# One core, decode attention for two caches: K queued one unit ahead of V, p.v two chunks behind the scores

## The chip, the cores and the metric

The kernel runs on one core of one Trainium2 chip. The metric is device time in microseconds: before, the median of three runs is 870.74 (870.53 to 872.84). The engines meant below are PE (matmul; PEld is its weight load), DVE (vector), ACT (scalar) and SP, which here only issues DMA transfers. A profile of one execution gives every instruction's start and duration, every DMA packet, and who released whom.

## The reference

Two attention blocks for a single query token, A over the whole cache and B over its last 4096 keys; their output rows are laid side by side:

```python
def _A_ref(x, k_cache, v_cache, wq, wo):          # x [1,1,512], caches [1,32,16384,128]
    q = (x @ wq).reshape(B, Sq, Hq, Dh).transpose(0, 2, 1, 3)
    scores = jnp.einsum("bhqd,bhkd->bhqk", q, k) * (Dh ** -0.5)
    p = softmax(scores, axis=-1)
    o = jnp.einsum("bhqk,bhkd->bhqd", p, v)
    return o.transpose(0, 2, 1, 3).reshape(B, Sq, Hq * Dh) @ wo
# _B_ref: the same with k_cache[:, :, Sk - W:], v_cache[:, :, Sk - W:], W = 4096
```

There are 32 heads of 128 in both, each with its own K and V. In bf16 one head of A has 4 MB of K and 4 MB of V, one head of B 1 MB of each; each wq and each wo has 4 MB. Every byte of K and V is used once.

## The kernel before

**Units and chunks.** The work is cut into 40 units. A unit is one head of A or four heads of B, so that it always has 128 keys on each of the 128 partitions: 4 MB of K and 4 MB of V. After every four heads of A comes the unit of B with the same four heads. A unit has two chunks of 64 keys a partition (U = 64); a chunk of B has two pieces, one for each of its two heads.

**Work on one chunk.** `_mult` (L144, DVE) multiplies K with the broadcast query into `prod`. `_add` (L156, DVE) adds the two halves of the head dimension. `_red` (L169, PE, eight matmuls with an identity) sums those further into PSUM. `_softmax` reduces the last eight columns (L181, DVE) and takes the exponential with its sum (L185, ACT). `_pv` (L201, PE) runs 64 small matmuls of p with V, and one with the sums (L210). When a head is through, its "fins" follow: reciprocal (L225, DVE), scaling (L227, ACT), a turn into a column (L239, PE), and after every fourth head a cast (L250, DVE) and the four matmuls with wo (`_fin_out`, L256, PE).

**Order on the engines.** Each engine runs its instructions in program order. The main loop emits for chunk c: the multiply of c, the softmax of c-1, the add of c, fins of earlier heads, the red of c, and then the p.v of chunk c-1. From the last two chunks on, p.v is put off: those of the last three chunks follow the red of the last one, with fins between.

**Order of the transfers.** All large loads are issued by SP, in the order of one list, `_Loads`, which emits the next load once its pool has a free buffer in program order. On the chip SP waits at the head of the queue until the readers of the buffer's old contents are done; all that is listed behind waits too. There are two buffers for K (`kt`, which also take both wq), two for V (`vt`), two for wo. A buffer of K is given back by the unit's second multiply, one of V by the p.v of its second chunk, one of wq by the q matmuls (L99), one of wo by `_fin_out` of its eighth head. The list runs

```
wqA, K0, V0, woA(0), K1, V1, K2, V2, wqB, woB(0), K3, V3, K4, V4, ...
```

so K and V of a unit stand together. A wo tile holds 1 MB for eight heads; A's is listed behind V of head 0, 8, 16, 24, B's behind V of A's head 2, 10, 18, 26. At the end K of the last unit, which is B's, goes ahead of the last V of A, and the last of the four V transfers of that unit is cut in two. x of A and of B is loaded on ACT's queue (L78), and DVE broadcasts both (L81) before its first multiply. The chunk with number 6 is preceded by the q matmuls of B.

Of the kernel before, what the change touches and what calls it, by code (L numbers as in the profile page):

```python
# [9 lines left out]
BF16 = mybir.dt.bfloat16  # L10
P = 128
# [5 lines left out]
G = 4  # L17
# [52 lines left out]
class _Unit:  # L70
    kt = vt = None
# [9 lines left out]
        cx.o(nc.vector.tensor_copy(st.xb[:, c, :], xT[:, c : c + 1].broadcast_to([P, P])))  # L81


def _load_wq(nc, cx, st):
    D, N = st.wq.shape
    KC = D // P
    st.wq_t = cx.kt_pool.tile([P, KC, N], BF16, tag="kt", name="wq_t")
    cx.o(nc.sync.dma_start(out=st.wq_t[:, :, :], in_=st.wq.rearrange("(p c) f -> p c f", c=KC)))


def _q(nc, cx, st):

    D, N = st.wq.shape
    KC = D // P
    st.qall = cx.singles.tile([P, N], BF16, tag=f"qall{st.name}", name=f"qall{st.name}")
    for j in range(N // 512):
        q_ps = cx.red_pool.tile([P, 512], F32, tag="red", name="q_ps")
        for c in range(KC):
            cx.o(nc.tensor.matmul(  # L99
                q_ps[:, :],  # L100
                lhsT=st.xb[:, c, :],
                rhs=st.wq_t[:, c, j * 512 : (j + 1) * 512],
                start=(c == 0),
                stop=(c == KC - 1),
            ))
        cx.o(nc.scalar.copy(st.qall[:, j * 512 : (j + 1) * 512], q_ps[:, :]))  # L106
    cx.loads.release("kt")


def _load_wo(nc, cx, st, i):  # L110

    t = cx.wo_pool.tile([P, 2, G * st.DN], BF16, tag="wo", name="wo_t")
    st.wo_t[i] = t
    n = 2 * G * DH
    cx.o(nc.sync.dma_start(  # L115
        out=t[:, :, :],
        in_=st.wo[i * n : (i + 1) * n, :].rearrange("(g p j) f -> p g (j f)", g=2, j=G),
    ))


def _load_kv(nc, cx, unit, which, cut_last=1):
    pool, tag = (cx.kt_pool, "kt") if which == "k" else (cx.vt_pool, "vt")
    t = pool.tile([P, unit.keys, DH], BF16, tag=tag, name=tag)
    setattr(unit, tag, t)
    st = unit.st
    view = st.k_view if which == "k" else st.v_view
    L = st.W // P
    n = len(unit.heads)
    for i, h in enumerate(unit.heads):
        src = view[h].rearrange("(p l) d -> p l d", p=P)  # L130
        cuts = cut_last if i == n - 1 else 1
        w = L // cuts
        for c in range(cuts):
            cx.o(nc.sync.dma_start(  # L134
                out=t[:, i * L + c * w : i * L + (c + 1) * w, :],
                in_=src[:, c * w : (c + 1) * w, :],
            ))


def _mult(nc, cx, ch):  # L140
    ch.prod = cx.prod_pool.tile([P, U, DH], BF16, tag="prod", name="prod")
    for k0, n, st, h, _, _ in ch.pieces:
        q = st.qall[:, h * DH : (h + 1) * DH]
        cx.o(nc.vector.tensor_tensor(  # L144
            out=ch.prod[:, k0 : k0 + n, :],
            in0=ch.unit.kt[:, ch.k0 + k0 : ch.k0 + k0 + n, :],
            in1=q.rearrange("p (o d) -> p o d", o=1).broadcast_to([P, n, DH]),
            op=ALU.mult,
        ))
    if ch.last_of_unit:  # L150
        cx.loads.release("kt")


def _add(nc, cx, ch):
    ch.half = cx.half_pool.tile([P, U, DH // 2], BF16, tag="half", name="half")
    cx.o(nc.vector.tensor_tensor(  # L156
        out=ch.half[:, :, :],
        in0=ch.prod[:, :, 0 : DH // 2],
        in1=ch.prod[:, :, DH // 2 : DH],
        op=ALU.add,  # L160
    ))
# [16 lines left out]
def _softmax(nc, cx, ch):  # L178

    sc = cx.small.tile([P, U], F32, tag="sc", name="sc")  # L180
    cx.o(nc.vector.tensor_reduce(out=sc[:, :], in_=ch.red[:, :, :], axis=AX.X, op=ALU.add))  # L181
    ch.p = cx.small.tile([P, U], BF16, tag="p", name="p_sb")
    ch.cs = cx.small.tile([P, len(ch.pieces)], F32, tag="cs", name="cs")
    for i, (k0, n, _, _, _, _) in enumerate(ch.pieces):
        cx.o(nc.scalar.activation(  # L185
            out=ch.p[:, k0 : k0 + n],
            in_=sc[:, k0 : k0 + n],
            func=ACT.Exp,
            scale=SCALE,
            accum_out=ch.cs[:, i : i + 1],  # L190
        ))


def _pv(nc, cx, ch, i):

    k0, n, st, h, first, last = ch.pieces[i]
    if first:
        st.o_ps[h] = cx.pso_pool.tile([1, DH + 1], F32, tag="o", name="o_ps")
    o_ps = st.o_ps[h]
    for c in range(n):  # L200
        cx.o(nc.tensor.matmul(  # L201
            o_ps[0:1, 0:DH],
            lhsT=ch.p[:, k0 + c : k0 + c + 1],
            rhs=ch.unit.vt[:, ch.k0 + k0 + c, :],
            start=(first and c == 0),
            stop=(last and c == n - 1),
            skip_group_check=True,
        ))
        if c == 0:
            cx.o(nc.tensor.matmul(  # L210
                o_ps[0:1, DH : DH + 1],
                lhsT=ch.cs[:, i : i + 1],
                rhs=cx.ones_col[:, 0:1],
                start=False,
                stop=last,
                skip_group_check=True,
            ))
    if ch.last_of_unit and i == len(ch.pieces) - 1:
        cx.loads.release("vt")
# [52 lines left out]
def kernel(  # L272
# [14 lines left out]
    nc = tc.nc  # L287
# [4 lines left out]
    cx = _Ctx()  # L292
    cx.o = _Order(tc)
    cx.out = out
    pool = lambda name, bufs, **kw: ctx.enter_context(tc.tile_pool(name=name, bufs=bufs, **kw))
# [12 lines left out]
    ld = cx.loads = _Loads()  # L308
# [19 lines left out]
    def problem(name, x, k_cache, v_cache, wq, wo, sk0, W, at):  # L328
        st = _Problem()
        st.name, st.x, st.wq, st.wo, st.W, st.at = name, x, wq, wo, W, at  # L330
        st.H = k_cache.shape[1]
        st.DN = wo.shape[1]
        st.k_view = k_cache[0, :, sk0 : sk0 + W, :]
        st.v_view = v_cache[0, :, sk0 : sk0 + W, :]
        st.out_ps = cx.psout_pool.tile([1, st.DN], F32, tag=f"out{name}", name=f"out{name}")
        st.wo_t, st.o_ps, st.orow = {}, {}, {}
        return st

    stA = problem("A", A_x, A_k_cache, A_v_cache, A_wq, A_wo, 0, SkA, 0)
    stB = problem("B", B_x, B_k_cache, B_v_cache, B_wq, B_wo, SkB - WB, WB, A_wo.shape[1])  # L340


    units = []
# [4 lines left out]
    chunks = []  # L348
    for i, (st, heads) in enumerate(units):
        u = units[i] = _Unit()  # L350
# [4 lines left out]
        for k0 in range(0, u.keys, U):  # L355
            pieces, at = [], 0
            while at < U:
                h, off = heads[(k0 + at) // L], (k0 + at) % L
                n = min(U - at, L - off)
# [3 lines left out]
        chunks += u.chunks  # L363


    ld.add("kt", lambda: _load_wq(nc, cx, stA))
    n = len(units)
    for i, u in enumerate(units):
        if i < n - 1:
            ld.add("kt", lambda u=u: _load_kv(nc, cx, u, "k"))  # L370
        if i == n - 2:
            ld.add("kt", lambda: _load_kv(nc, cx, units[n - 1], "k"))
        ld.add("vt", lambda u=u, c=(2 if i == n - 1 else 1): _load_kv(nc, cx, u, "v", c))
        if i == G - 2:
            ld.add("kt", lambda: _load_wq(nc, cx, stB))
        per = 2 * G
        if u.st is stA and u.heads[0] % per == 0:
            ld.add("wo", lambda b=u.heads[0] // per: _load_wo(nc, cx, stA, b))
        if u.st is stA and u.heads[0] % per == 2:
            ld.add("wo", lambda b=u.heads[0] // per: _load_wo(nc, cx, stB, b))  # L380

    _load_x(nc, cx, stA)
    _load_x(nc, cx, stB)
# [3 lines left out]
    fins = []  # L387


    def fin_pe():  # L390
        for f in list(fins):
            s, st, h = f
            if s == 1:
                _fin_col(nc, cx, st, h)
                f[0] = 2 if h % G == G - 1 else 9
            elif s == 3:
                _fin_out(nc, cx, st, h)
                f[0] = 9
        fins[:] = [f for f in fins if f[0] != 9]

    def fin_dve():
        for f in fins:
            s, st, h = f
            if s == 0:
                _fin_row(nc, cx, st, h)
                f[0] = 1
            elif s == 2:
                _fin_cast(nc, cx, st, h)
                f[0] = 3

    def pv(ch):
        for i, (_, _, st, h, _, last) in enumerate(ch.pieces):
            _pv(nc, cx, ch, i)
            if last:
                yield [0, st, h]

    prev = None
    waiting = []
    tail_from = len(chunks) - 3
    for c, ch in enumerate(chunks):  # L420
        if c == 2 * (G - 1):
            _q(nc, cx, stB)
        _mult(nc, cx, ch)
        if prev is not None:
            _softmax(nc, cx, prev)
            waiting.append(prev)
        _add(nc, cx, ch)
        fin_dve()
        fin_pe()
        _red(nc, cx, ch)  # L430
        if c <= tail_from:
            while waiting:
                fins += pv(waiting.pop(0))
        prev = ch
    _softmax(nc, cx, prev)
    waiting.append(prev)
# [40 lines left out]
```

## Time and profile before

| what | value |
|---|---|
| median of three runs | 870.74 us |
| the profiled execution | 869.08 us |
| its span, first to last instruction | 867.4 us |
| granted TensorE clock, mean | 0.838 |
| busy: DVE, PE, PEld, ACT | 588.4, 567.8, 390.7, 64.8 us |
| HBM read | 352.32 MB |
| share of the 16 DMA engines that SP's transfers took | 95.9% |
| idle of DVE before the multiply, ended by A's K | 208.0 us |

A row of a group gives busy time, then the mean duration of one instruction in nanoseconds, then the idle time before it and who ended it. The row of a window gives its ends, the busy time of each engine, then the granted clock, the mean share of the DMA engines in use and GB/s; packets are counted where they start. "SPq" is SP's queue, an instruction there is the issue of a transfer. Times are counted from the span's start.

### The profile page before, as it was taken

The page shows a single profiled execution, that of the slowest core. Times are in us where ns is not written, and L with a number is a line of the kernel's source. Part 1 is how long each engine was busy: PE and PEld are TensorE (multiplying, and loading weights), DVE is VectorE, ACT ScalarE, POOL GpSimd, SP SyncE. Part 2 cuts the span into 40 slices and gives each one's busy share as a digit, 9 for nine tenths or more (in the row PEclk, how much of TensorE's full clock was granted, in tenths as well). Part 3 has the DMA queues.
Part 4 walks back from the last instruction along what each step waited for, and adds up shares of the span by engine and source line. Part 5 has one row for each costly group of instructions (what it writes and reads, how often), then busy time and mean ns, then how long its engine had stood idle before and what let it go on. Part 6 is the DMA issues. An engine that isn't in the chain of part 4 may idle for free.

```text
span 867.4 us, 13704 instructions
## 1 busy us (share of the span) xinstructions
PE 567.8 (65%) x6336; PEld 390.7 (45%) x6336; DVE 588.4 (68%) x344; ACT 64.8 (7%) x275; POOL 0.8 (0%) x8
## 2 busy tenths in 40 slices
PE   3466585766665765676855758577757575667678
PEld 1154263544443544444633536344544354444446
DVE  0666486769557695777865768666955769577791
ACT  2000200000010000100000000000001000010001
POOL 0000000000000000000000000000000000000000
PEclk9688897988977888888977879788897788888888
DMA  9999999999989999999989999999998999999980
GB/s 387 435 428 417 428 436 426 417 424 417 437 360 434 427 413 439 418 425 422 433 371 433 408 426 426 428 414 430 401 440 362 422 426 418 439 411 416 431 359 2
DMA packets 21389, 353.20 MB, mean 407 GB/s; under 512 B 2514, under 2 KB 2516, under 8 KB 4820
## 3 DMA queue, kind: packets, MB, share of 16 engines
q1 hardware_dynamic: 21044, 352.33, 95.9%
q8 instruction: 49, 0.80, 0.4%
q10 hardware_dynamic: 288, 0.00, 0.0%
q14 instruction: 8, 0.07, 0.0%
HBM read 352.32 MB, written 0.00 MB: 406 GB/s over the span
## 4 chain that ended last, share of the span: by engine, by line
DMA 56%; DVE 18%; PE 17%; issue 7%; SPq 1%; ACT 0%; DVEq 0%; ACTq 0%
DMA kt<-in_A_k_cache_dram 53%; PE o_ps L201 9%; DVE prod L144 9%; DVE half L156 7%; PE red L169 6%; DMA xTB<-in_B_x_dram 3%; DVE sc L181 2%; PE outB L256 2%; SPq L134 1%; PE outA L256 1%; SPq L115 0%; DVE oc L250 0%; PE oc_ps L239 0%; DVE recip L225 0%; PE o_ps L210 0%
## 5 line engine op out<-in xcount | busy, mean ns | idle before, releaser
L144 DVE TENSOR_TENSOR prod<-kt,qallA 128x8192 bf16<-128x8192 bf16 x64 | 283.0, 4422 | 208.6 <-DMA kt<-in_A_k_cache_dram 208.0
L201 PEld LDWEIGHTS <-p_sb 128*1 128x1 bf16 x5120 | 296.7, 85 | 42.8 <-issue 42.7
L201 PE MATMUL o_ps<-vt,p_sb 128*1 128x128 bf16 x5120 | 314.1, 222 | 1.7 <-DMA vt<-in_A_v_cache_dram 1.7
L169 PE MATMUL red<-half,ident 128*128 128x512 bf16 x640 | 203.2, 475 | 126.7 <-DVE half L156 126.7
L156 DVE TENSOR_TENSOR half<-prod 128x4096 bf16<-128x4096 bf16 x80 | 182.5, 2282 | 0.0
L169 PEld LDWEIGHTS <-ident 128*128 128x128 bf16 x640 | 68.4, 114 | 225.5 <-issue 178.9
L185 ACT ACTIVATE p_sb<-sc 128x64 bf16<-128x64 f32 (+1 forms) x96 | 23.5, 244 | 654.6 <-DVE sc L181 654.6
L144 DVE TENSOR_TENSOR prod<-kt,qallB 128x4096 bf16<-128x4096 bf16 x32 | 71.9, 2287 | 0.3
L181 DVE TENSOR_REDUCE sc<-red 128x64 f32<-128x512 f32 x80 | 54.8, 685 | 12.8 <-PE red L169 12.6
L256 PEld LDWEIGHTS <-oc 128*1 128x1 bf16 x64 | 5.3, 101 | 126.5 <-DVE oc L250 75.9
L256 PE MATMUL outA<-wo_t,oc 128*1 128x512 bf16 x32 | 14.1, 591 | 69.3 <-DVE recip L225 59.6
L256 PE MATMUL outB<-wo_t,oc 128*1 128x512 bf16 x32 | 14.1, 590 | 45.6 <-DVE oc L250 45.6
L239 PE MATMUL oc_ps<-one,orow 1*32 1x1 bf16 x256 | 16.3, 171 | 35.6 <-ACT orow L227 35.6
L239 PEld LDWEIGHTS <-orow 1*32 1x32 bf16 x256 | 11.5, 110 | 49.7 <-ACT orow L227 42.1
L227 ACT ACTIVATE orow<-o_ps,recip 1x128 bf16<-1x128 f32 x64 | 22.2, 357 | 111.0 <-DVE recip L225 111.0
L225 DVE RECIPROCAL recip<-o_ps 1x1 f32<-1x1 f32 x64 | 9.1, 150 | 28.4 <-PE o_ps L201 28.1
L210 PE MATMUL o_ps<-ones_col,cs 128*1 128x1 f32 x192 | 19.0, 168 | 0.0
L185 ACT ACTIVATION_READ_ACCUMULATOR p_sb<-sc 128x1 f32 x96 | 17.9, 186 | 0.0
L99 PE MATMUL q_ps<-wq_t,xbA 128*128 128x512 bf16 x32 | 8.4, 430 | 13.5 <-DVE xbA L81 13.5
L210 PEld LDWEIGHTS o_ps<-ones_col,cs 128*1 128x1 f32 x192 | 14.1, 87 | 1.7 <-issue 1.7
L99 PEld LDWEIGHTS <-xbA 128*128 128x128 bf16 x32 | 3.5, 108 | 18.0 <-DVE xbA L81 13.7
L99 PE MATMUL q_ps<-wq_t,xbB 128*128 128x512 bf16 x32 | 8.2, 378 | 4.7 <-ACT qallB L106 4.7
(17 smaller groups left out, 19.6 us busy)
## 6 DMA issues: line engine op xcount, KB each, us to landing
kt<-in_A_k_cache_dram SPq DMA_DIRECT2D x32, 4096.0 KB, 23.5
vt<-in_A_v_cache_dram SPq DMA_DIRECT2D x32, 4096.0 KB, 16.7
kt<-in_B_k_cache_dram SPq DMA_DIRECT2D x32, 1024.0 KB, 19.8
vt<-in_B_v_cache_dram SPq DMA_DIRECT2D x31, 1024.0 KB, 10.0
wq_t<-in_A_wq_dram SPq DMA_DIRECT2D x1, 4096.0 KB, 12.2
wo_t<-in_A_wo_dram SPq DMA_DIRECT2D x4, 1024.0 KB, 5.0
wq_t<-in_B_wq_dram SPq DMA_DIRECT2D x1, 4096.0 KB, 24.6
wo_t<-in_B_wo_dram SPq DMA_DIRECT2D x4, 1024.0 KB, 16.9
```

Source lines behind the costliest of these rows:

```text
L99: cx.o(nc.tensor.matmul(q_ps[:, :], lhsT=st.xb[:, c, :], rhs=st.wq_t[:, c, j * 512 : (j + 1) * 512], start=(c == 0), stop=(c == KC - 1),))
L144: cx.o(nc.vector.tensor_tensor(out=ch.prod[:, k0 : k0 + n, :], in0=ch.unit.kt[:, ch.k0 + k0 : ch.k0 + k0 + n, :], in1=q.rearrange("p (o d) ...
L156: cx.o(nc.vector.tensor_tensor(out=ch.half[:, :, :], in0=ch.prod[:, :, 0 : DH // 2], in1=ch.prod[:, :, DH // 2 : DH], op=ALU.add,))
L169: cx.o(nc.tensor.matmul(ch.red[:, :, :], lhsT=cx.ident[:, :], rhs=ch.half[:, :, b * W : (b + 1) * W], start=(b == 0), stop=(b == nb - 1),))
L181: cx.o(nc.vector.tensor_reduce(out=sc[:, :], in_=ch.red[:, :, :], axis=AX.X, op=ALU.add))
L185: cx.o(nc.scalar.activation(out=ch.p[:, k0 : k0 + n], in_=sc[:, k0 : k0 + n], func=ACT.Exp, scale=SCALE, accum_out=ch.cs[:, i : i + 1],))
L201: cx.o(nc.tensor.matmul(o_ps[0:1, 0:DH], lhsT=ch.p[:, k0 + c : k0 + c + 1], rhs=ch.unit.vt[:, ch.k0 + k0 + c, :], start=(first and c == 0) ...
L210: cx.o(nc.tensor.matmul(o_ps[0:1, DH : DH + 1], lhsT=ch.cs[:, i : i + 1], rhs=cx.ones_col[:, 0:1], start=False, stop=last, skip_group_chec ...
L225: cx.o(nc.vector.reciprocal(recip[:, :], o_ps[0:1, DH : DH + 1]))
L227: cx.o(nc.scalar.activation(out=orow[:, :], in_=o_ps[0:1, 0:DH], func=ACT.Copy, scale=recip[0:1, 0:1]))
L239: cx.o(nc.tensor.matmul(st.oc_ps[32 * hp : 32 * hp + 32, j : j + 1], lhsT=orow_j[:, j, :], rhs=cx.one[0:1, 0:1], start=True, stop=True,))
L256: cx.o(nc.tensor.matmul(st.out_ps[0:1, :], lhsT=st.oc[:, j : j + 1], rhs=st.wo_t[i][:, g, j * st.DN : (j + 1) * st.DN], start=(h == G - 1 ...
```

## The change

The list of loads is made in a new order. K of unit i now stands ahead of V of unit i-1:

```
wqA, K0, K1, V0, K2, V1, wqB, K3, woA(0), V2, K4, woB(0), V3, K5, V4, ...
```

wqA takes a V buffer instead of a K buffer, so that K0 and K1 can be loaded at once; wqB still takes a K buffer, and `_q` gives back whichever it was. The wo loads move: A's tile stands behind K of A's head 3, 11, 19, 27, B's behind K of B's unit with heads 0, 8, 16, 24. V of the last two units is cut: the last A head's V into two loads of 2 MB, and the last transfer of the last B unit as before. In the main loop p.v waits until two chunks are in the list, so it runs for chunk c-2 after the red of c; after the loop two chunks are left instead of three, and the third runs at the loop's end after the last red, in the same place as before. The number of computing instructions is the same, and there is one transfer more.

```diff
-def _load_wq(nc, cx, st):
+def _load_wq(nc, cx, st, tag):
...
-    st.wq_t = cx.kt_pool.tile([P, KC, N], BF16, tag="kt", name="wq_t")
+    st.wq_tag = tag
+    pool = cx.kt_pool if tag == "kt" else cx.vt_pool
+    st.wq_t = pool.tile([P, KC, N], BF16, tag=tag, name="wq_t")
...
-    cx.loads.release("kt")
+    cx.loads.release(st.wq_tag)
...
-    ld.add("kt", lambda: _load_wq(nc, cx, stA))
+    ld.add("vt", lambda: _load_wq(nc, cx, stA, "vt"))
     n = len(units)
-    for i, u in enumerate(units):
-        if i < n - 1:
+    for i in range(n + 1):
+        if i == G - 1:
+            ld.add("kt", lambda: _load_wq(nc, cx, stB, "kt"))
+        if i < n:
+            u = units[i]
             ld.add("kt", lambda u=u: _load_kv(nc, cx, u, "k"))
-        if i == n - 2:
-            ld.add("kt", lambda: _load_kv(nc, cx, units[n - 1], "k"))
-        ld.add("vt", lambda u=u, c=(2 if i == n - 1 else 1): _load_kv(nc, cx, u, "v", c))
-        if i == G - 2:
-            ld.add("kt", lambda: _load_wq(nc, cx, stB))
-        per = 2 * G
-        if u.st is stA and u.heads[0] % per == 0:
-            ld.add("wo", lambda b=u.heads[0] // per: _load_wo(nc, cx, stA, b))
-        if u.st is stA and u.heads[0] % per == 2:
-            ld.add("wo", lambda b=u.heads[0] // per: _load_wo(nc, cx, stB, b))
+            per = 2 * G
+            if u.heads[0] % per == (3 if u.st is stA else 0):
+                ld.add("wo", lambda u=u, b=u.heads[0] // per: _load_wo(nc, cx, u.st, b))
+        if i:
+            ld.add("vt", lambda u=units[i - 1], c=(2 if i >= n - 1 else 1): _load_kv(nc, cx, u, "v", c))
...
-    tail_from = len(chunks) - 3
...
-        if c <= tail_from:
-            while waiting:
-                fins += pv(waiting.pop(0))
+        if len(waiting) > 1:
+            fins += pv(waiting.pop(0))
```

## The prediction

> **What bounds the kernel now.** I read the page first (span, engines, DMA rate, queues).
>
> ```profile
> span 867.4 us, 13704 instructions
> ...
> PE 567.8 (65%) x6336; PEld 390.7 (45%) x6336; DVE 588.4 (68%) x344; ACT 64.8 (7%) x275; POOL 0.8 (0%) x8
> ...
> GB/s 387 435 428 417 428 436 426 417 424 417 437 360 434 427 413 439 418 425 422 433 371 433 408 426 426 428 414 430 401 440 362 422 426 418 439 411 416 431 359 2
> ...
> q1 hardware_dynamic: 21044, 352.33, 95.9%
> q8 instruction: 49, 0.80, 0.4%
> ...
> HBM read 352.32 MB, written 0.00 MB: 406 GB/s over the span
> ```
>
> No engine is busy over 68%; the transfers fill 95.9% of the span. The kernel is a stream of 352.32 MB with three kinds of loss: slices at 360 to 371 GB/s, smaller dips, and a last slice that moves almost nothing. The second view, the waits of SP, says why the stream thins out: SP issues in order, and stands on buffers.
>
> ```profile
> SPq L134 <- PE o_ps L201: 617.6, 38, 26.3
> SPq L115 <- PE outA L256: 62.3, 3, 20.8
> SPq L134 <- DVE prod L144: 36.6, 5, 12.0
> ```
>
> A V load waits for the p.v matmuls that read its buffer (38 times), and three loads of A's wo wait for the out matmul. The SP timeline around the first of those three, then the windows (columns from the right: GB/s, DMA share, clock):
>
> ```profile
> 224.36 0.33 SPq L134 DMA_DIRECT2D vt<-in_A_v_cache_dram  x1
> 245.54 0.38 SPq L115 DMA_DIRECT2D wo_t<-in_A_wo_dram  x1
> 246.01 0.42 SPq L134 DMA_DIRECT2D kt<-in_A_k_cache_dram  x1
> ```
>
> ```profile
> 0.00:4.00 4.00, 0.00 (x0) 0.00 (x0) 0.00 (x0) 1.28 (x1) 0.77 (x8) 1.00 0.68 229
> ...
> 154.00:156.50 2.50, 2.32 (x18) 1.17 (x19) 0.14 (x1) 0.13 (x1) 0.00 (x0) 1.00 0.96 354
> ...
> 243.00:248.00 5.00, 4.36 (x18) 1.43 (x19) 5.00 (x5) 0.61 (x2) 0.00 (x0) 0.50 0.35 114
> ...
> 448.50:453.00 4.50, 4.12 (x17) 1.28 (x18) 4.50 (x5) 0.61 (x2) 0.00 (x0) 0.50 0.28 89
> ...
> 655.00:660.50 5.50, 4.66 (x19) 1.54 (x20) 5.23 (x5) 0.61 (x2) 0.00 (x0) 0.50 0.39 122
> ...
> 832.00:834.50 2.50, 2.12 (x12) 0.98 (x13) 2.50 (x2) 0.24 (x1) 0.00 (x0) 1.00 0.73 226
> 261.00:345.00 84.00, 53.25 (x614) 37.64 (x614) 60.87 (x32) 4.41 (x22) 0.00 (x0) 0.83 1.00 426
> 362.00:448.50 86.50, 56.73 (x673) 40.47 (x669) 65.36 (x34) 4.94 (x26) 0.00 (x0) 0.85 1.00 427
> 843.50:846.00 2.50, 0.00 (x0) 0.00 (x0) 2.50 (x3) 0.53 (x4) 0.00 (x0) 0.94 0.18 72
> 846.00:867.40 21.40, 17.55 (x238) 13.38 (x237) 2.10 (x9) 3.38 (x11) 0.00 (x0) 0.90 0.01 2
> ```
>
> Undisturbed, the stream runs at 427 GB/s (two windows of 84 and 86.5 us, with B's units and wo loads in them). From 224.7 to 245.5 SP issues nothing: the wo load heads its queue and K of the next head stands behind it. A window's loss is its length times (1 - rate / 427): 3.7 us at 243, 3.6 at 448.5, 3.9 at 655, so 11.2 us for the three. Nine short dips (the first is 154.0, the last 832.0; 0.4 and 1.2 us) lose 4.5 us together. After 846.0 no load moves, and 21.4 us of compute follow.
>
> **The change, part by part.** Durations per chunk of 64 keys, from the groups:
>
> ```profile
> L144 DVE TENSOR_TENSOR prod<-kt,qallA 128x8192 bf16<-128x8192 bf16 x64 | 283.0, 4422 | 208.6 <-DMA kt<-in_A_k_cache_dram 208.0
> L201 PE MATMUL o_ps<-vt,p_sb 128*1 128x128 bf16 x5120 | 314.1, 222 | 1.7 <-DMA vt<-in_A_v_cache_dram 1.7
> ...
> L156 DVE TENSOR_TENSOR half<-prod 128x4096 bf16<-128x4096 bf16 x80 | 182.5, 2282 | 0.0
> ...
> L181 DVE TENSOR_REDUCE sc<-red 128x64 f32<-128x512 f32 x80 | 54.8, 685 | 12.8 <-PE red L169 12.6
> ```
>
> and the chain of waits over the last two units (start, us, what):
>
> ```profile
> 791.50 24.89 DMA kt<-in_A_k_cache_dram
> ...
> 823.76 3.57 PE red L169 x8
> ...
> 846.45 3.18 PE red L169 x8
> 849.63 0.15 PE o_ps L201
> ...
> 849.81 3.60 PE o_ps L201 x64
> ...
> 860.72 1.77 PE o_ps L201 x31
> ...
> 864.78 0.58 ACT rowB L267
> ```
>
> One chunk costs DVE 4.42 + 0.69 + 2.28 = 7.4 us, a unit 14.8; PE about 3.6 (red) and 3.7 (p.v) a chunk. A 4 MB load takes 4.19 MB / 427 = 9.8 us, so K and V of a unit take 19.6: DVE has 4.8 us to spare a unit.
>
> *Order of loads and p.v lag, mid-stream.* Nothing is computed more or less; what moves is when each buffer comes free against the turn of its next load. Call T the landing of K(u). The new queue is K(u), V(u-1), K(u+1), V(u), K(u+2), V(u+1). K(u+2) needs the second multiply of unit u: T + 7.4 + 4.4 = T+11.8. Its turn comes after three loads, T+29.4: 17.6 us ahead. V(u+1) needs p.v of unit u-1's second chunk, now run after the red of iteration 2u+1: T + 14.8 + 3.6 + 3.7 = T+22.1; its turn is T+39.2: 17.1 ahead. In the old order K(u), V(u), K(u+1), V(u+1), K(u+2), V(u+2), the load V(u+2) waits for p.v of chunk 2u+1, which runs after the red of the iteration that K(u+1) opens at T+19.6: T + 19.6 + 7.4 + 3.6 + 3.7 = T+34.3, with the turn at T+39.2. Only 4.9 us ahead, and any fin or out work on PE eats it: these are the short dips. So 4.5 us go.
>
> *New wait.* PE meets p.v of chunk 2u in iteration 2u+2, at T + 19.6 + 7.4 + 3.6 = T+30.6, and V(u) lands at T+29.4: no wait. Behind a B unit, whose chunks DVE can start before its last K piece lands (at T-4.8), PE is there about 5 us ahead of V and waits. Behind that matmul stand the next red, then DVE's reduction one iteration later; that iteration opens with the next K, T+19.6, and PE is through by T+21, so nothing on DVE is late.
>
> *wo loads.* They now come with K of A's heads 3, 11, 19, 27 and B's units 0, 2, 4, 6, three heads later than before for the loads that stalled. The out matmul that frees the buffer (head 7, 15, 23) runs about a unit before the load is reached. The three stalls go: 11.2 us. If that cover failed, a stall would be worth 3.7 us again. Their 1 MB each still streams (2.5 us), no more bytes than now.
>
> *Start.* First in the queue are wqA, K0, K1, V0 instead of wqA, K0, V0, wo.
>
> ```profile
> 1.24 21.91 DMA xTB<-in_B_x_dram
> ```
> ```profile
> 34.96 0.33 SPq L134 DMA_DIRECT2D kt<-in_A_k_cache_dram  x1
> ```
>
> DVE's first work needs B's x, which landed at 23.15. The second multiply then ends at 34.9, and K2 can be issued there; four loads of 9.8 us from 2 us on last until 41: 6 us ahead. wqB (a K buffer, after the fourth multiply at 49.7) and K3 (after the sixth, 64.5) have turns at 61 and 70: covered, K3 by 6. B's K0 waits for q of B and has wo and V queued ahead. I take the start at nothing; bounds: no gain, a loss of 4 us if x lands a load later (below).
>
> *The stream's end.* From the bytes: 352.32 / 0.427 = 825.1 us, plus the first window's loss 4.0 x (1 - 229/427) = 1.9 and the uneven last 2.5 us, 2.1: 829.1. From the losses: 846.0 - 11.2 - 4.5 = 830.3. I take the middle, **829.7**.
>
> *The tail.* K of A's last unit landed at 791.50 + 24.89 = 816.4; from there to the end 51.0 us ran: four chunks on DVE (30.0 to 846.4), red, p.v of three chunks, the fins. All of that follows K, not V, and the new program orders chunks 77 to 79 as the old one does. In the old order K(B), V, V followed this K; now V of the unit before does too: 16.8 MB instead of 12.6, 39.3 us at 427 instead of 29.6. So this K lands at 829.7 - 39.3 = 790.4, and the end is 790.4 + 51.0 = **841.4**. V must keep up: the last p.v began 860.6 - 816.4 = 44.2 after K, so now at 834.6, and the last V piece lands at 829.7; p.v of chunk 77 began 33.2 after K, now 823.6, with its V half landed 9.8 before the end, at 819.9; chunk 76, moved one iteration later, comes after the third red, 790.4 + 3 x 7.4 + 3.6 = 816.2, and the first half of its V lands 14.7 before the end, at 815.0 (the whole load, at 819.9, would be 3.7 late). The cut adds one issue of 0.4 us on SP, which is ahead. The tail after the loads is 11.7 us where it was 21.4.
>
> *Sum.* Span 867.4 to 841.4, -26.0: 16.3 from the stream, 9.7 from the tail. The profiled execution took 869.08, 1.7 over its span, and the median, 870.74, is 1.7 over that: 841.4 + 1.7 + 1.7 = **844.8**.
>
> **A rule of the skill.** The Trainium skill, "DMA: Bandwidth & Descriptors", section Specifications, gives a limit of about 358 GB/s of HBM for a core and a fabric ceiling of 435 GB/s. By the first the stream would need 984 us and no order of loads could help; the trace, at 406 over the whole span, contradicts it. By the ceiling it would need an estimated 810 us, an end about 15 us earlier than mine.
>
> **Rivals.**
>
> (a) The short dips are not late issues but uneven DMA engines (49 instruction packets go through the same engines) and stay. For: they are shallow, 330 to 387 GB/s, not 100. Against: they begin where a V issue was late. Stream end 846.0 - 11.2 = 834.8, + 11.7, + 3.4 = 849.9.
>
> (b) The last V load is late instead: its buffer needs p.v of chunk 75, about 17 us before the stream's end, turn 9.8 before it. If the tail stays at 21.4: 829.7 + 21.4 + 3.4 = 854.5. Against: 7 us of lead and 4.9 of slack behind.
>
> (c) x of B lands with the second K, a load (9.8 us) later; K2 is issued at 44.7 against 41: about 4 us, 848.8. Against: the first three issues keep their order.
>
> (d) The stream runs better than in the quiet windows.
>
> ```profile
> 664.00:688.00 24.00, 14.31 (x157) 9.24 (x155) 14.45 (x10) 1.41 (x6) 0.00 (x0) 0.79 1.01 436
> ```
>
> At 436 throughout, 808.1 instead of 825.1: 17 us less, about 828. B's 8 KB rows and the instruction loads, in every group of units, speak against.
>
> (e) Slower: V behind the next K holds PE in order, with the next red behind it and DVE's reduction behind that, so that K's buffer comes late. It decides once PE's wait pushes DVE by more than the 17.6 us of lead; each microsecond beyond is one of idle stream, in 40 units. To lose the 26.0 and 2.6 more it takes 0.7 us a unit, PE late by 18.3 us: at least 873.4. Against: the longest wait found above is about 5.
>
> **How the numbers follow.** Forecast 0.66 (own range 841 to 848), (a) 0.11, (b) 0.07, (c) 0.07, (d) 0.03, (e) 0.03, and 0.03 that it stays within 0.3% (2.6 us, about what this measurement tells from no change). The range 840 to 853 leaves out (b), (d), (e), and no change. Faster: all but (e) and no change, 0.94.
>
> **What would show it.** In the changed profile: no SP wait of L115 on the out matmul; no slice under 400 GB/s between the first and the last; loads ending near 830; V loads issued 15 us and more before their turn; 11 to 12 us from the last load to the end; the last A unit's K landing near 790 and 51 us to the end from it. DVE idle on PE, a slice near 360, or a rate under 420 in quiet windows would make it wrong.

## The result, and the profile after

The changed kernel takes 844.49 us, the median of four runs (844.37 to 844.52), against 870.63 before, here the median of four runs too; the ratio is 0.9699 (0.9675 to 0.9723). The forecast was 844.8. The profiled execution took 844.37 us with a span of 842.7, so 24.7 us of span have gone, where the sum had 26.0. The page of the changed kernel:

```profile
span 842.7 us, 13703 instructions
...
GB/s 384 437 422 429 430 420 434 429 436 424 416 437 430 428 428 417 436 426 422 438 426 424 435 412 437 430 425 437 425 415 433 433 427 431 415 432 433 428 390 155
...
q1 hardware_dynamic: 21188, 352.33, 98.2%
...
q8 instruction: 49, 0.80, 0.4%
...
L203 PE MATMUL o_ps<-vt,p_sb 128*1 128x128 bf16 x5120 | 335.4, 230 | 56.4 <-DMA vt<-in_A_v_cache_dram 56.4
```

The slices of 360 to 371 GB/s are gone; 390 in the last but one is left, where the prediction had asked for none under 400. Lines have moved by two (L201 of before is L203). SP's waits, and the windows that answer to those of before:

```profile
SPq L136 <- PE o_ps L203: 339.8, 36, 12.2
SPq L136 <- DVE prod L146: 294.8, 37, 11.8
```

```profile
362.00:448.50 86.50, 63.78 (x734) 47.19 (x732) 62.10 (x37) 5.66 (x28) 0.00 (x0) 0.86 1.01 429
...
813.00:817.50 4.50, 3.11 (x43) 2.36 (x40) 4.50 (x4) 0.71 (x3) 0.00 (x0) 1.00 0.76 295
...
826.00:832.50 6.50, 6.50 (x121) 6.37 (x118) 0.38 (x3) 1.07 (x6) 0.00 (x0) 1.00 0.55 224
...
833.00:842.70 9.70, 6.35 (x91) 4.70 (x89) 0.47 (x3) 2.12 (x5) 0.00 (x0) 1.00 0.00 0
```

No wait of a wo load on the out matmul is left; SP still waits for p.v and for the multiply, but now the queue is full meanwhile. The undisturbed rate is as before (429 against 427).

The lead can be read from the time between a V load's issue and its landing, here in the kernel before and in the changed one:

```profile
vt<-in_A_v_cache_dram SPq DMA_DIRECT2D x32, 4096.0 KB, 16.7
```
```profile
vt<-in_A_v_cache_dram SPq DMA_DIRECT2D x31, 4096.0 KB, 28.0
```

Less the 9.8 us of the load itself, that is 6.9 us ahead of its turn before and 18.2 now; the prediction had 4.9 and 17.1.

What the forecast did not have is in the second and third row of the windows: a stall at 813.0, and 6.5 us at the end in which the stream runs at half its rate with a DMA share of 0.55. By the windows the loads end at 832.5, not 829.7, and 10.2 us follow, not 11.7. (A window counts a packet where it starts; the last completion mark of a load is at 833.1, and at 845.9 in the kernel before.) The chain of waits at the end:

```profile
766.69 27.06 DMA kt<-in_A_k_cache_dram
...
823.10 1.89 PE red L171 x8
...
840.14 0.57 ACT rowB L269
```

K of A's last head lands at 793.8, 3.4 us later than the sum put it, and 49.0 us run from there to the end instead of 51.0.

### The profile page after: what moved, and what is told of

It reads as the page before. It is cut to its first block, busy times and chain, and to the rows that moved or that the text cites. A ratio compares the mean times of both kernels' runs of the same rounds, so it can differ in the third digit from the quotient of the medians.

```text
span 842.7 us, 13703 instructions
## 1 busy us (share of the span) xinstructions
PE 576.0 (68%) x6336; PEld 410.8 (49%) x6336; DVE 587.3 (70%) x344; ACT 64.7 (8%) x275; POOL 0.8 (0%) x8
## 4 chain that ended last, share of the span: by engine, by line
DMA 65%; DVE 20%; issue 7%; PE 6%; SPq 0%; ACT 0%; DVEq 0%
DMA kt<-in_A_k_cache_dram 52%; DVE prod L146 13%; DMA vt<-in_A_v_cache_dram 7%; DMA kt<-in_B_k_cache_dram 6%; DVE half L158 6%; PE o_ps L203 4%; PE red L171 1%; DVE sc L183 1%; DVE recip L227 0%; PE outB L258 0%; PE oc_ps L241 0%; SPq L136 0%; PE outA L258 0%; ACT orow L229 0%; ACT rowB L269 0%
## 5 line engine op out<-in xcount | busy, mean ns | idle before, releaser
L203 PE MATMUL o_ps<-vt,p_sb 128*1 128x128 bf16 x5120 | 335.4, 230 | 56.4 <-DMA vt<-in_A_v_cache_dram 56.4
L203 PEld LDWEIGHTS <-p_sb 128*1 128x1 bf16 x5120 | 317.4, 89 | 44.2 <-issue 44.2
L227 DVE RECIPROCAL recip<-o_ps 1x1 f32<-1x1 f32 x64 | 9.0, 148 | 18.3 <-PE o_ps L203 18.3
L101 PEld LDWEIGHTS <-xbA 128*128 128x128 bf16 x32 | 3.6, 114 | 18.1 <-DVE xbA L81 8.5
L258 PE MATMUL outB<-wo_t,oc 128*1 128x512 bf16 x32 | 8.2, 379 | 0.3 <-DVE oc L252 0.3
L258 PE MATMUL outA<-wo_t,oc 128*1 128x512 bf16 x32 | 8.2, 379 | 0.0
L101 PEld LDWEIGHTS <-xbB 128*128 128x128 bf16 x32 | 3.1, 96 | 10.1 <-issue 7.2
```

The costliest lines, as they stand in the source:

```text
L101: cx.o(nc.tensor.matmul(q_ps[:, :], lhsT=st.xb[:, c, :], rhs=st.wq_t[:, c, j * 512 : (j + 1) * 512], start=(c == 0), stop=(c == KC - 1),))
L203: cx.o(nc.tensor.matmul(o_ps[0:1, 0:DH], lhsT=ch.p[:, k0 + c : k0 + c + 1], rhs=ch.unit.vt[:, ch.k0 + k0 + c, :], start=(first and c == 0) ...
L227: cx.o(nc.vector.reciprocal(recip[:, :], o_ps[0:1, DH : DH + 1]))
L258: cx.o(nc.tensor.matmul(st.out_ps[0:1, :], lhsT=st.oc[:, j : j + 1], rhs=st.wo_t[i][:, g, j * st.DN : (j + 1) * st.DN], start=(h == G - 1 ...
```

## Experiments

The theory on record is one of leads: the stream stops when an issue comes after its turn, and the end follows the last K of A. The trace of the changed kernel adds a second one to test: the DMA engines drift apart.

**The wo loads alone.** In the kernel before, the two old wo entries are taken out of the list, and a wo load stands between K and V of its unit:

```diff
+        if u.heads[0] % per == (3 if u.st is stA else 0):
+            ld.add("wo", lambda u=u, b=u.heads[0] // per: _load_wo(nc, cx, u.st, b))
```

> The kernel before, with nothing but the wo loads moved: A's behind K of heads 3, 11, 19, 27, B's behind K of its units 0, 2, 4, 6. Theory of leads (a stall is an issue that comes after its turn, each costs once): the three stalls of 11.2 us go, the short dips of 4.5 us and the tail of 21.4 us stay: 870.6 - 11.2 = 859.4, within 857 to 862, no wait of the wo load on the out matmul. Rival, drift: the stalls also let the slower DMA engines catch up; without them the dips grow and the gain is under 8 us, above 862.6.

Measured: 866.5 us (865.3 to 867.6; ratio 0.9934, 0.9916 to 0.9953), a gain of about 5.8 (4.1 to 7.3) and not 11.2; the spans of the two profiled executions differ by 3.8. The range was missed on the rival's side, but not for the rival's reason. Where the first wo load had stood, the SP timeline and the window now show:

```profile
225.29 0.37 SPq L134 DMA_DIRECT2D kt<-in_A_k_cache_dram  x1
255.16 0.33 SPq L134 DMA_DIRECT2D vt<-in_A_v_cache_dram  x1
```

```profile
253.00:258.50 5.50, 5.01 (x69) 3.66 (x66) 2.27 (x4) 0.72 (x2) 0.00 (x0) 1.00 0.69 247
419.50:426.00 6.50, 5.51 (x75) 4.35 (x74) 6.47 (x5) 0.35 (x2) 0.00 (x0) 1.00 0.96 352
459.50:463.50 4.00, 3.51 (x40) 2.16 (x38) 0.76 (x3) 0.72 (x2) 0.00 (x0) 1.00 0.86 307
```

A V load waits 28.3 us there for the p.v of a B unit and is late by itself: at 427 GB/s the three windows lose 2.3, 1.1 and 1.1 us. The third of them is where the second wo load had stood; a V load waits 26.8 us there. So at two of the three places the wo load had stood in front of another late load, and its stall was worth only what it added to that.

**The lag alone.** In the kernel before:

```diff
-        if c <= tail_from:
-            while waiting:
-                fins += pv(waiting.pop(0))
+        if len(waiting) > 1:
+            fins += pv(waiting.pop(0))
```

> The kernel before, with nothing but p.v run two chunks behind. Theory of leads: a V buffer now comes free 22.1 us after the landing of the K behind which its new load stands, 19.6 us of transfers after it; with 0.8 us from issue to data a unit takes 21.2 us instead of 19.6, so about 60 us more for 40 units: 920 to 945. Rival: lag alone costs nothing, since PE and ACT have idle time: 868 to 873.

Measured: 969.1 us (ratio 1.1113, 1.1096 to 1.113), over the range. SP's wait for p.v, 617.6 us in the kernel before, and the window from 200 to 800 us, with 364 GB/s:

```profile
SPq L134 <- PE o_ps L201: 733.0, 38, 32.1
```

```profile
200.00:800.00 600.00, 350.21 (x4043) 247.66 (x4044) 374.14 (x215) 33.80 (x163) 0.00 (x0) 0.79 0.87 364
```

The rival is out: in the old order p.v is what V's buffer waits for, and PE's idle time is no cover. The loss, 97 us, is over the 60 worked out; the hand sum priced all 40 units like plain A units, and what B's units, the fins and the lower granted clock (0.797 against 0.838) add was not taken apart. Its 0.8 us from issue to data is on the short side, too: in the kernel before, the wo load issued at 245.54 has its first packet at 246.58.

**The new order alone.** The changed kernel with the old loop end:

```diff
-        if len(waiting) > 1:
-            fins += pv(waiting.pop(0))
+        if c <= tail_from:
+            while waiting:
+                fins += pv(waiting.pop(0))
```

> The changed kernel with its new order of loads, but p.v one chunk behind and the old end (the last three chunks' p.v after the last red). Theory: PE meets p.v of a unit 9 to 11 us before its V lands and holds the next red, DVE's last add moves by about 4 us at the end, and mid-stream DVE finishes a unit at best 0.5 us late, so B's units, where V lands later still, starve the stream somewhere: 848 to 863, that is 4 to 18 us over the changed kernel. Rival: the order of loads alone does it all, within 1 us of 844.5. Second rival: the held red stops DVE in every unit and K's buffers come late, over 870.

Measured: 857.0 us (ratio 0.9825, 0.9808 to 0.9841), 12.5 over the changed kernel, inside the theory's range and against both rivals. It is lost at two ends, not in the middle. At the start PE stands 18.1 us on V of the third unit with q of B queued behind it, K of B's first unit waits for that q, and the stream dries up (windows, the first of them there, the others at the end):

```profile
93.00:97.50 4.50, 2.17 (x23) 2.17 (x23) 1.82 (x1) 0.00 (x0) 0.00 (x0) 0.50 0.42 115
817.00:821.00 4.00, 3.36 (x39) 2.21 (x36) 3.24 (x4) 0.36 (x1) 0.00 (x0) 1.00 0.80 291
830.00:837.00 7.00, 3.72 (x13) 1.21 (x13) 3.27 (x4) 0.54 (x4) 0.00 (x0) 0.62 0.42 171
837.00:855.30 18.30, 14.99 (x230) 12.95 (x226) 1.65 (x8) 3.37 (x11) 0.00 (x0) 0.96 0.00 1
```

That is 4.5 x (1 - 115/427) = 3.3 us. At the end PE holds the reds behind p.v that has no V yet, as the chain of waits shows:

```profile
778.72 28.63 DMA vt<-in_A_v_cache_dram
...
807.69 5.26 PE o_ps L203 x63
812.95 1.83 PE red L171 x8
...
833.28 3.57 PE red L171 x8
```

The last red begins at 833.3 (823.1 in the changed kernel), and 18.3 us follow the loads instead of 10.2. The second rival had the wait right and its effect wrong:

```profile
DVE sc L183 <- PE red L171: 167.1, 32, 15.9
```

DVE stands 167.1 us in all on held reds (4.4 in the changed kernel), yet the stream runs at 428 GB/s from 97.5 to 817.0: the lead of the issues covers it. Neither half of the change is worth its share alone: the order without the lag gains 15.3 us on the kernel before, little more than half, and the lag without the order costs 97 us.

**The cut of the last A head's V** is taken back:

```diff
-c=(2 if i >= n - 1 else 1): _load_kv(nc, cx, u, "v", c))
+c=(2 if i >= n else 1): _load_kv(nc, cx, u, "v", c))
```

> The changed kernel with the V load of A's last head whole (no halves). By the prediction, p.v of chunk 76 then waits 3.7 us for the second half, with the last red behind it: 844.5 plus 2 to 3.7 us, since the changed profile has about 1 us between that red's operand and PE. Rival: there is slack elsewhere in the end and nothing changes, within 0.5 us of 844.5.

Measured: 850.5 us (ratio 0.9752, 0.9738 to 0.9767), 6.0 more, over the range. In its chain of waits p.v of chunk 76 starts when the whole load lands, at 823.5, and then runs at a lower granted clock, 0.69 from 823.5 to 829.0, with 5.2 us for 63 matmuls instead of 3.6:

```profile
795.55 27.98 DMA vt<-in_A_v_cache_dram
...
823.82 5.16 PE o_ps L203 x63
828.98 1.83 PE red L171 x8
```

In the changed kernel the last red began at 823.1; here it begins at 829.0, 5.9 us later.

**Does the end follow K?** In the changed kernel K of A's last head comes in two halves:

```diff
-            ld.add("kt", lambda u=u: _load_kv(nc, cx, u, "k"))
+            ld.add("kt", lambda u=u, c=(2 if i == n - 2 else 1): _load_kv(nc, cx, u, "k", c))
```

> The changed kernel with K of A's last head loaded in two halves of 2 MB. Theory (the end follows that K): in the changed profile K landed at 793.8 and 49 us followed. With halves the first multiply starts a half-load, 4.9 us, earlier, until V sets the end: the last V piece landed about 833, and with 16 keys' p.v (1 us) and the fins (4.9) that is 839 instead of 842.7. So 844.5 - 3 to 5: 839.5 to 841.5. Rival: V sets the end already, within 1 us of 844.5.

Measured: 844.09 us (843.95 to 844.83; 0.9665, 0.9641 to 0.9689): no change, as the rival had it, though V's *last* load isn't the reason. The chain of waits left K for V of the head before:

```profile
777.61 26.30 DMA vt<-in_A_v_cache_dram
...
804.24 5.69 PE o_ps L203 x63
809.93 1.83 PE red L171 x8
```

PE stands on that load until 803.9 with the red of chunk 77 behind it. So both waits were to go, and V of that head is cut too:

```diff
-c=(2 if i >= n - 1 else 1): _load_kv(nc, cx, u, "v", c))
+c=(2 if i >= n - 2 else 1): _load_kv(nc, cx, u, "v", c))
```

> The changed kernel with the last three large A loads in halves: K of A's last head, V of the A head before it, V of the last A head (the last is so already). With K alone in halves nothing moved, since PE stood on the whole V load before it (landed 803.9) with the next red queued behind. Theory (two waits of equal length, both have to go): PE then starts chunk 74 with the first V half at about 799, DVE's chain runs 4 to 5 us earlier, V's last load is issued about 5 us earlier (810 instead of 815) and the 1.4 us stall of the stream there goes; the second half of the last A head's V, at about 822, sets the end: 842 to 843. Rival: the last V landings alone set the end: within 0.5 us of k_cut's 844.1.

Measured: 844.51 us (844.25 to 844.83; 0.9658, 0.9634 to 0.9683): no change again. What the theory said of the way came true: V's last load is issued at 809.8 instead of 814.9, and the stall is gone. The gain isn't there; the windows:

```profile
813.00:817.50 4.50, 2.60 (x10) 1.09 (x11) 4.50 (x4) 0.36 (x1) 0.00 (x0) 0.55 1.00 424
823.50:833.50 10.00, 10.00 (x150) 8.31 (x148) 1.23 (x5) 1.25 (x6) 0.00 (x0) 1.00 0.55 223
```

The stretch at half rate has grown from 6.5 to 10 us, and the loads end no earlier (last mark at 833.8, against 833.1). With a DMA share of 0.76 in the old stall, some DMA engines ran dry there and others never did; those others set the end.

**Why half the engines are late.** In the trace every transfer leaves 16 completion marks, taken here as one from each DMA engine. Time from the first to the last mark (the spread), in us, for the transfers that end nearest to the times on top, and the largest of all:

```
kernel   q8 packets   100 us   200   400   600   800   largest
before        49        1.9    2.4   2.2   2.5   2.5     3.5
changed       49        1.9    3.3   4.8   7.7   9.5     9.5
kv_cut        49        2.1    3.3   5.2   8.0   9.9    10.1
half_pv       29        1.6    1.6   3.2   4.7   6.3     6.5
pv2           31        1.7    2.0   3.6   5.2   6.8     6.8
```

In the changed kernel the marks of eight engines stay within about 4 us to the end, those of the other eight step back by about 1.5 us one after another, six times round; up to 185 us the number that have stepped is the number of instruction packets on q8 so far. Before, by this reading, each stall and dip let them catch up; in no_lag the stall at 93.0 brings the spread from 1.9 to 0.5 us. The first test leaves out every second key's p.v:

```diff
-    for c in range(n):
+    for c in range(0, n, 2):
...
-            stop=(last and c == n - 1),
+            stop=(last and c == n - 2),
```

> The changed kernel, leaving out every second key's p.v matmul (all loads stay, the output is another). It asks why the last 6.5 us of the changed kernel's stream run on about half the DMA engines (share 0.55 at 826.0 to 832.5, 224 GB/s). Theory: half of the engines also fetch PE's instructions (49 packets of 16 KB on q8), lose about 1.5 us for each fetch, and nothing lets them catch up while the stream never runs dry. Half the p.v takes 5120 of PE's 12672 instructions away: 28 to 31 instruction packets, and the half-share stretch at the end shrinks to 3 to 4 us; the last A unit's K lands 1.5 to 2.5 us earlier; 832 to 838 in all, p.v of the end being shorter too. Rival: the unevenness comes from the loads themselves: the half-share stretch stays at 6 us or more.

Measured: 837.7 us (one run), 29 packets, both in the theory's ranges. K of A's last head landed at 791.0, 2.8 us earlier and so a little more than forecast, and the largest spread fell from 9.5 to 6.5. The time by itself says little, since PE's work at the end is shorter too. The stretch at half rate did not shrink, 6.5 us at a share of 0.52 in this window:

```profile
823.50:830.00 6.50, 5.86 (x91) 4.76 (x89) 0.69 (x5) 1.96 (x6) 0.00 (x0) 1.00 0.52 211
```

That number met the rival, and misled: in the changed kernel the stall at 813 had let 3 us of the spread go, here there is no stall (428 GB/s from 805 to 815). Beside kv_cut, which has none either, 10 us became 6.5. The second test means to give some engines more bytes; V of the first unit comes in four transfers of 8 partitions and one of 96:

```diff
+        for r in range(0, rows8 * 8, 8):
+            cx.o(nc.sync.dma_start(out=t[r : r + 8, :, :], in_=src[r : r + 8, :, :]))
+        if rows8:
+            cx.o(nc.sync.dma_start(out=t[rows8 * 8 :, :, :], in_=src[rows8 * 8 :, :, :]))
+            continue
...
```

> The changed kernel with V of the first unit loaded as four pieces of 8 partitions and one of 96, so that, if an 8-row transfer runs on 8 engines alone, these get four rows of 32 KB more than the others, 4.9 us at 1.2 us a row. Theory of uneven engines: the unevenness at the end, 6 to 9 us between the two halves, starts with a handicap. If the 8 are the ones that do not fetch instructions, it shrinks by 4.9 us, the last K lands about 2.4 us earlier and the time falls to 841.5 to 843; if they are the ones that do, it grows and the time rises to 846 to 848. Rival: an 8-row transfer is spread over all 16, or the unevenness costs nothing: within 0.7 us of 844.5.

Measured: 867.7 us (0.993, 0.9903 to 0.9958). No theory had that. While these pieces ran, the stream fell to a third with a DMA share of 1, as the windows show:

```profile
35.00:40.00 5.00, 1.85 (x5) 0.73 (x6) 4.96 (x4) 0.35 (x2) 0.00 (x0) 0.73 1.01 125
40.00:50.00 10.00, 5.31 (x13) 1.44 (x10) 9.96 (x5) 0.35 (x2) 0.00 (x0) 0.50 1.06 147
```

It says nothing on the drift; why these pieces are slow stays open. The third test takes the instructions away and keeps the work; the fins take both rows of the result, and the turn into a column adds the two diagonal blocks:

```diff
-    for c in range(n):
+    for c in range(0, n, 2):
         cx.o(nc.tensor.matmul(
-            o_ps[0:1, 0:DH],
-            lhsT=ch.p[:, k0 + c : k0 + c + 1],
-            rhs=ch.unit.vt[:, ch.k0 + k0 + c, :],
+            o_ps[0:2, 0 : 2 * DH],
+            lhsT=ch.p[:, k0 + c : k0 + c + 2],
+            rhs=ch.unit.vt[:, ch.k0 + k0 + c : ch.k0 + k0 + c + 2, :],
...
-        cx.o(nc.tensor.matmul(
-            st.oc_ps[32 * hp : 32 * hp + 32, j : j + 1],
-            lhsT=orow_j[:, j, :],
-            rhs=cx.one[0:1, 0:1],
-            start=True,
-            stop=True,
-        ))
+        for b in range(2):
+            cx.o(nc.tensor.matmul(
+                st.oc_ps[32 * hp : 32 * hp + 32, j : j + 1],
+                lhsT=orow_j[:, b, j, :],
+                rhs=cx.ident[0:2, b : b + 1],
+                start=(b == 0),
+                stop=(b == 1),
+            ))
...
```

> The changed kernel with two keys to each p.v matmul: two columns of p are the weights, 256 columns of V stream through, the wanted sums are the two diagonal blocks of a 2 x 256 result, and the turn into a column adds them. Loads and result are the same; PE has 32 x 2 instead of 64 x 2 instructions a chunk and 8 instead of 4 small matmuls a head: 12672 - 5120 + 512 = 8064, that is 31 or 32 instruction packets instead of 49. Theory (eight DMA engines lose 1.5 us for each packet they fetch and the slowest of them sets the end): 17.5 packets fewer over 8 engines are 3.3 us less on the slowest, the last landing moves from 833 to about 830 and the time to 841 to 842, if 256 columns cost PE no more than twice 128. Rival: the slow engines are slow for another reason: within 0.6 us of 844.5. Second rival: the wider matmuls or the added fins lengthen PE's chain at the end: over 845.

Measured: 842.59 us (842.59 to 843.12; 0.9655, 0.9636 to 0.9674), with 31 packets; the last landing, by its mark, went from 833.1 to 830.6. PE pays nothing for the wider matmuls, as the page shows (323.4 us in all against 335.4):

```profile
q8 instruction: 31, 0.51, 0.2%
...
L203 PE MATMUL o_ps<-vt,p_sb 128*2 128x256 bf16 x2560 | 323.4, 286 | 53.0 <-DMA vt<-in_A_v_cache_dram 53.0
```

The direction and the 830 are as forecast, the time 0.6 us over the range. With the halves added:

> Both: two keys to a p.v matmul, and the last three large A loads in halves. With halves alone the 1.4 us stall before the last V went and nothing was won, since the slow engines never stood still in it. Theory: the same here, 841 to 842, within 0.7 us of pv2. Rival: with the slow engines less far behind, the halves' earlier start of the last chunks counts: 1 to 3 us below pv2.

Measured: 842.07 us (841.52 to 842.52; 0.9646, 0.9627 to 0.9665), within 0.7 us of pv2 as expected. On one chip with the changed kernel:

> The changed kernel unaltered, on one chip with the next, so that the two can be set side by side: 844 to 845.

> Two keys to a p.v matmul and the halves, once more: 2.0 to 2.8 us under the changed kernel on the same chip. Rival: the difference between the earlier calls was one of chips, under 0.8 us here.

Measured: 844.72 us (844.66 to 844.97) and 841.83 us (841.57 to 842.65): 2.9 us faster than the changed kernel, just over the range, and the fastest of the versions that leave nothing out.

## Why the prediction was right, and where it was not

**Bound and direction: right.** The stream sets the time; with K ahead of V the issues come before their turns and the middle runs at the undisturbed rate. The order's own working is borne out from both sides: in the old order p.v's place decides (lag_only), and in the new one the wo loads and the short dips cost nothing: from 4 to 813 us the stream runs at 428 GB/s. That answers three rivals. (a): the dips are gone although the engines drift further apart than before. (d): the rate is not 436. (e): PE's waits do not stop the stream. And (c): K2 was issued at 34.24, no later than before.

**The stream's 16.3 us: 13.5 measured** (846.0 to 832.5; 12.8 by the last marks). The split was wrong. "The three stalls go: 11.2 us" was the term that a single edit gave to 5.8: a late V load stood behind the wo load, and only the new order removes that one. In the middle the sum of both terms held because the change makes both edits. The bottom-up figure, bytes by the undisturbed rate, needed no split. It counted every engine's bytes alike, though, and the last landing is that of the slowest engine: the half-rate window loses 6.5 x (1 - 224/427) = 3.1 us, and the stall at 813.0 another 1.4, where the sum had 2.1 for an uneven end. Those 2.4 us are most of the 3.4 by which the end worked out from the bytes, 829.1, was missed (829.7 by 2.8); the rest was not taken apart. The last K is late in the same way, by 3.4 us: its first mark comes 9.5 us before its last. (The sum also divided SP's bytes alone by a rate that counts the 0.9 MB of instruction packets, 2 us; the middle at 428 and not 427 gives about that back.)

**The new wait: sized for an even stream.** PE's wait for V was put at about 5 us behind B units and harmless; there are 56.4 us of it, up to 9.6 at a time, and it does no harm in the middle:

```profile
PE o_ps L203 <- DMA vt<-in_A_v_cache_dram: 56.4, 12, 9.6
```

DVE waits 4.4 us for reds in all (12.6 before). But the p.v lag was priced at nothing of its own. Without it 12.5 us are lost: it is what keeps PE from meeting V early at the first q of B and at the end.

**The last V's "7 us of lead", rival (b): half came true.** Its buffer's p.v ended at 814.9 instead of the 812.7 that "about 17 us before the stream's end" makes, and the first engines came to its turn at 813, about 7 us before the 819.9 of an even stream; so the stall at 813.0, 4.5 x (1 - 295/427) = 1.4 us. As kv_cut shows, the end did not pay for it. The other half, a tail that stays at 21.4 us, did not come.

**The tail's 9.7 us: 11.2 measured** (21.4 to 10.2). The step "51.0 us from the last K" was 49.0: one red ran in 1.9 us instead of 3.2, and DVE's wait of 0.7 for a fin is gone. That the end follows K alone was too simple. K, the V load before it, and the last V landings lie within a few microseconds of one another, which is why halves of the first two changed nothing.

**The sum: 1.3 us short in the span**, made good by the last step: 1.7 us from the profiled execution to the median, copied from the kernel before, was 0.1 here. That the forecast of 844.8 came within 0.3 us is therefore luck in part: a stream 2.8 us too short, a tail 1.5 too long and a last step 1.6 too long cancel.

**The cut: right in kind, 3.7 us for 6.0.** The landing of the whole load was taken from an even stream, and p.v was priced at full clock; the landing came 3.6 us later than the sum had it, and p.v took 1.6 us longer.

## What to carry to other kernels

Where one in-order queue feeds a stream, price an edit by the lead of every issue behind the one that is moved: a stall can hide a second one, and taking away the first then pays only the difference. Order and lag belong together: load first what frees its buffer early, and let its consumer run late enough that no in-order engine meets data that is still queued behind. A stream that never runs dry ends with its slowest DMA engine, so here the number of instructions counted too: by the marks, their fetches ride on the same engines.

## What had not been expected of the hardware

By the pattern of the completion marks, instruction packets of 16 KB fall on eight of the sixteen DMA engines in turn, and each sets its engine back by about 1.5 us against the others; 49 of them made 9.5 us between the first and the last engine of a transfer, 31 made 6.8. The Trainium skill, "Runtime: NRT & Kernel Launch", section "Instruction fetch mechanics", has blocks of 16 KiB or 256 instructions, and this agrees (12672 PE instructions, 49 packets). It calls the cost of crossing a block mostly hidden; no run here measures that cost on PE, but on the transfers it was not hidden. Which eight engines fetch, and whether they change from one program to another, was not tried.

A transfer confined to 8 partitions with rows of 32 KB ran far below the others: a stream at 125 to 147 GB/s.
